# Feed-forward products of a spectral-mixing and SwiGLU kernel: float32 products with block sums and Strassen, against three float32r products of 12-bit parts in stripes of 512 tokens

## Chip, core and metric

The kernel runs on one core of one Trainium2 chip. The metric is the device time of one execution in microseconds (us). Three runs of the kernel before gave 2791.26, 2792.60 and 2793.78 us, so its median is 2792.6 us.

Engine names are those of the profile: PE is TensorE (matrix products), PEld its weight loads, DVE is VectorE, ACT is ScalarE, POOL is GpSimd, SP is SyncE, which only issues DMAs here.

## What is computed

```python
batch, seq, dim = 8, 3008, 256
d_ff = 1536
X = np.fft.rfft(x, axis=1)                       # x: (8, 3008, 256) float32
y = np.fft.irfft(X * (filt_r + 1j * filt_i)[None], n=seq, axis=1)
x2 = y.astype(np.float32).reshape(8 * 3008, 256)  # 24064 tokens
g = x2 @ w_gate                                   # 256 x 1536
h = g * (1.0 / (1.0 + np.exp(-g))) * (x2 @ w_val)
out = (h @ w_out).astype(np.float32)              # 1536 x 256
```

The three weight matrices arrive as 64-bit floats and are turned into 32-bit ones on the chip.

## The kernel before

**Spectral part.** For each of the 8 batches the transforms are short products with tables of sines and cosines, with twiddle and filter factors between them. Batch 0 runs first, alone, in stages written out by hand: `stage1_first`, `turn`, `stage2a`, `stage2b`, `stage3` (L896 to L1026). Its result is needed in four chunks (`NCHUNK`), and the feed-forward part starts when chunk 0 is there. Each later batch is transformed while the feed-forward part of the batch before it runs; its products are bursts of small matmuls: `quads` (tile wqa, L727), `fours` (wqb L819 there, wqc L807 home) and `back` (wpd, L1043). Batch 1 still uses an older path (`stage1`, `stage2a`, `stage2b`).

**Feed-forward part.** `Group` (L1091) is one chunk of a batch with a third of the hidden units: 96 groups. The tokens of a chunk stand in four classes, and the weights in four blocks. The hidden products are taken of sums of token classes and of weight blocks (`P`, `Q`, `A`, `B`, `E` in `product`, L1118, matmuls at L1125): 26 products for the gate half and 26 for the value half, each a matmul of 128x128 weights with 188 columns of float32. DVE, ACT and POOL form the sums before and after (`f`, `c`, `D`, `x`, `y`, `m`, `l`, `s`, `e`). The output product is a Strassen scheme: seven products of 128x128 with 376 columns, each over two blocks (`project`, L1223, 14 matmuls a group), with sums of hidden tiles (`S`, on POOL, L312 and L315) before and additions into the output (`o`, DVE L312) behind.

**Weights.** `round_half` (L386) turns one half of a weight block from 64-bit to 32-bit floats with DVE, ACT and POOL operations of 128x256 elements (DVE: L395, L398, L418, L422). `Preparation` spreads these operations over the first groups. The finished sums of weights are kept in DRAM and a third of them is loaded again for every group (`reload_weights`, tile wt_t from w_all).

**Order.** All engines run their instructions in program order; `pin` keeps that order. The order inside a group is the hand-written list `SCHEDULE`: each token is one operation of this group, of the one before it, or one step of a spectral piece. DMAs are nearly all issued by SP, in program order.

Two helpers hide what an operation is for: `add` (L312) and `sub` (L315) issue sums on the engine that they are given, `negated_sum` (L319) one DVE operation. A matmul of float32 shows as two MATMUL records in the trace.

Of the kernel before, what the change touches and what calls it, by code (L numbers as in the profile page):

```python
# [12 lines left out]
FP32 = mybir.dt.float32  # L42
U32 = mybir.dt.uint32
# [7 lines left out]
NM = DFF // 128  # L51
NJ = NM // 2
# [6 lines left out]
NH = 4  # L59
NW = 2 * NH  # L60
NCHUNK = 32 // NW
TH = NH * NR
RP = 96
NT = 3
NG = 3
JB = NJ // NG
TQ = TH // 2
NB = 8
# [9 lines left out]
WO = {1: 0, 7: 1, 2: 2, 3: 3, 5: 4, 6: 5, 4: 6}  # L78
HID = {1: 0, 6: 6, 4: 2, 2: 3, 5: 4, 7: 1, 3: 5}

SCHEDULE = """
Q0 o3' z1.o' t4.2' W2 b0 f0 S00' S01' i0 b1 b2 x0.o' t0.0 x1.o' i1 Q1 P0 t0.1 x2.o' P3 x3.o' f1 t4.3'
W1 x4.o' S10' x03 S11' D01 i2 i3 i4 s13 b3 x5.o' P1 o1 b4 t0.2 o2 z0.o c1 i5 A13 g1 c0 S20' Q2  # L90
S21' g0 y01 m13 t1.0 h0 f2 s01 W6 t1.1 h1 x23 D02 P2 o6 D12 A01 t0.3 i6 c2 i7 B13 i8 g2 i9 n3' m01
i10 S30' t1.2 i11 x02 W7 S31' g13 y12 y02 B01 h13 o7 t1.3 t2.0 s02 s12 g01 h2 b5 Q3 t2.1 h01 e12
A02 y23 W4 e02 b6 y03 m02 g3 A12 o4 z2.o t2.2 E12 m12 B02 t2.3 l12 e13 b7 E02 u12 g02 t3.0 h3 s23
l02 B12 v12 E13 t3.1 h02 u02 A23 n2 l13 g12 v02 W5 s03 e23 h12 e01 m23 A03 o5 z3.o u13 E23 t3.2 m03
v13 E01 l23 e03 t3.3 t4.0 l01 u23 B23 v23 u01 E03 n1 t4.1 v01 g23 B03 l03 W3 h23 g03 u03 h03 v03
""".split()
KS = (-1, 0, 1, 2)

LAST = """
S00 S01 W1 S20 S21 S10 S11 W2 o1 W5 o2 S30 S31 W6 o5 o6 W4 W7 q4 o4 z2.o x0.o x1.o x2.o x3.o x4.o x5.o  # L100
o7 W3 o3 z1.o X0.o X1.o X2.o X3.o X4.o X5.o
""".split()
FILTER_AT = ("f1", "P0", "Q2", "h0")
BLOCKS = (0, 1, 3, 2)
PAIRS = ((0, 1), (1, 2), (2, 3), (0, 2), (1, 3), (0, 3))
PAIRS_USED = ((1, 3), (0, 1), (0, 2), (1, 2), (2, 3), (0, 3))
ORDER = [t for t in SCHEDULE if t[0] in "PQABE"]
VIA_SBUF = {t[1:] for t in SCHEDULE if t[0] == "x" and t[1:].isdigit()}, \
    {t[1:] for t in SCHEDULE if t[0] == "y"}
SLOT = {p: i for i, p in enumerate(ORDER)}  # L110
SUM = {f"{z}{i}{j}": 6 * e + n for e, z in enumerate("ABE") for n, (i, j) in enumerate(PAIRS)}
NPR = len(ORDER)

LATER = N1 - 32

PIECES = ((0, 7), (7, 14), (14, 20), (20, 26))

def dft_tables():
# [45 lines left out]
    for t in range(NS):  # L168
        u, at = divmod(t, 4)
        for e in range(2):  # L170
# [11 lines left out]
    thc = th - np.where(n2 < 32, 0.0, 1.0)[:, None, None] * 2 * np.pi * s / (2 * N1)  # L182
    c, sn = np.cos(thc), np.sin(thc)
    turned = np.zeros((2, N2, NS, 2, NQ))
    turned[0, :, :, 0] = c.transpose(0, 2, 1)
    turned[1, :, :, 0] = sn.transpose(0, 2, 1)
    turned[0, :, :, 1] = (-sn * sg).transpose(0, 2, 1)
    turned[1, :, :, 1] = (c * sg).transpose(0, 2, 1)
    turned = turned.reshape(128, NS, 128).transpose(2, 1, 0)

    pairs = np.arange(128).reshape(2, N2).T.ravel()
    later = np.stack([de[:, :, 0], turned[:, :, pairs]], 2)
    f32 = np.float32
    wf = np.pad(wf.reshape(NR, NK), ((0, 0), (0, 128 - NK)))
    return (wf.astype(f32), wi.reshape(NK, NR).astype(f32),
            back.astype(f32), quad.astype(f32), four.astype(f32), np.ascontiguousarray(de).astype(f32),
            np.ascontiguousarray(later).astype(f32))
# [3 lines left out]
def kernel(  # L201
# [11 lines left out]
    wf_host, wi_host, back_host, quad_host, four_host, de_host, later_host = dft_tables()  # L213
# [6 lines left out]
    later_dram = nc.inline_tensor(later_host, name="later_tbl").ap()  # L220
    unit_dram = nc.inline_tensor(np.eye(128, dtype=np.float32), name="unit_tbl")

    def pool(name, bufs, space=None):
# [4 lines left out]
    xpool = pool("xp", 2)  # L228
    t1pool = pool("t1", 2)
    t4pool = pool("t4", 2)  # L230
    ypool = pool("yp", 2)
    wdpool = pool("wdram", 1, DRAM)
    wps = pool("wps", NB, PSUM)

    wf_t = cpool.tile([NR, 128], FP32)
    wi_t = cpool.tile([NK, NR], FP32)

    wt_t = cpool.tile([128, NPR, 2, 128], FP32)
    y_t = cpool.tile([128, 3 * len(PAIRS), TQ], FP32)

    lent = cpool.tile([128, 14 * NV * C], FP32)
    wt_1 = lent[:, 0:NPR * 256].rearrange("p (s z f) -> p s z f", z=2, f=128)
    places = {"t2": (0, 2, 1), "f": (2, 2, 2), "tb": (6, 3, 1), "p": (9, 2, 1), "q": (11, 1, 1),
              "g": (12, 2, 1)}

    def lend(tag, u):

        first, count, units = places[tag]
        a = (first + u % count * units) * NV * C
        return lent[:, a:a + units * NV * C].rearrange("p (i c) -> p i c", c=C)  # L250

    fours = {"x": (0, 2, 2), "f": (0, 4, 1), "y": (4, 2, 1), "g": (6, 2, 1), "e": (8, 2, 1),
             "t": (10, 2, 1), "tb": (12, 1, 1)}
# [7 lines left out]
    def weights_of(b, k, g):  # L261
        return wt_1 if b == 0 and k < NT and g == 1 else wt_t

    dram_tiles = [wdpool.tile([2 * NS, N2, C], FP32, name=f"d{1 + i % 2}_{i // 2}")
                  for i in range(4)]
    quads_dram = [wdpool.tile([64, N2, C], FP32, name=f"quads_{i}") for i in range(2)]
    turned_dram = [wdpool.tile([16, 128, C], FP32, name=f"turned_{i}") for i in range(2)]
    yt_dram = [wdpool.tile([128, 3 * len(PAIRS), TQ], FP32, name=f"yt_{k}") for k in range(NT)]
# [55 lines left out]
    def weight_halves():  # L324
# [8 lines left out]
        def hid(g, i):  # L333
            for z in range(2):
                yield cols[z][JB * g + i // 2][:, i % 2], ("hid", g, i, z)
# [1254 lines left out]
```

## Time and profile before

| what | value |
|---|---|
| median of 3 runs | 2792.6 us |
| profiled execution, span from first to last instruction | 2788.6 us (4.0 us under the median) |
| granted TensorE clock, mean | 0.997 of full speed |
| busy: PE, DVE, POOL, ACT | 99%, 75%, 59%, 54% |
| first feed-forward product starts | 76.1 us |
| PE matmuls of line L1125 (hidden products), records | 9984 in the six largest groups |
| DMA | 608.47 MB, mean 218 GB/s |
| weights loaded again (wt_t from w_all) | 174 loads of 896 KB, 174 of 768 KB |

The span is the time of one profiled execution, and the sums of the prediction are made against it. A group of instructions in the page is given as line, engine, operation, output and input tiles, shape and count, then busy time (overlaps counted once) and mean duration of one in ns. In the timeline the first column is the start in us, the second the length of a merged run of equal instructions. Instructions of one engine overlap a little, so that what one costs in a dense stream is the distance of starts, not its duration.

### The profile page before, as it was taken

The numbers are of one execution on the slowest core, as the hardware profiler recorded it, in microseconds if no ns is written. First come the engines' busy times: TensorE is split into PE (matmuls) and PEld (weight loads), VectorE is DVE, ScalarE is ACT, GpSimd is POOL, SyncE is SP. The second block draws the span as 40 slices with busy tenths as digits, with TensorE's granted clock in tenths as the row PEclk, the third lists the DMA queues.
The fourth block names the chain that finished last, engine by engine and source line by source line (L and its number), as shares of the span: only waits on it lengthen the run. The fifth ranks groups of instructions, "written<-read, shape, count | busy, mean of one in ns | idle before, by whom it ended". The sixth has DMA issues, their size and how long they took to land.

```text
span 2788.6 us, 51410 instructions
## 1 busy us (share of the span) xinstructions
PE 2748.3 (99%) x16952; PEld 2249.3 (81%) x16952; DVE 2081.7 (75%) x4703; ACT 1514.6 (54%) x4086; POOL 1647.4 (59%) x1801
## 2 busy tenths in 40 slices
PE   8999999999999999999999999999999999999998
PEld 6777887888878888788878888878887888888886
DVE  7888777777687777777778777777777777676666
ACT  5776454555555555555555555555554555555553
POOL 4786576566545665556654566555655566555554
PEclk9999999999999999999999999999999999999999
DMA  8688877878676776777767777668767677655543
GB/s 216 218 273 267 282 240 243 265 243 263 205 211 208 253 244 190 212 238 229 247 184 233 220 249 223 207 194 264 243 213 201 215 239 237 183 156 147 156 137 83
DMA packets 383488, 608.47 MB, mean 218 GB/s; under 512 B 197118, under 2 KB 266652, under 8 KB 383048
## 3 DMA queue, kind: packets, MB, share of 16 engines
q1 hardware_dynamic: 364410, 574.18, 65.9%
q10 hardware_dynamic: 16174, 25.50, 3.6%
q0 software_dynamic: 2640, 5.51, 0.7%
q8 instruction: 137, 2.24, 0.3%
q14 instruction: 127, 1.04, 0.1%
HBM read 484.45 MB, written 118.12 MB: 216 GB/s over the span
## 4 chain that ended last, share of the span: by engine, by line
PE 89%; DVE 3%; POOL 2%; ACT 1%; DMA 1%; issue 1%; SPq 0%; POOLq 0%; DVEq 0%; ACTq 0%
PE wa L1125 25%; PE wk L1125 17%; PE wA L1223 16%; PE we L1125 12%; PE wG L1223 8%; PE wF L1223 4%; PE wpd L1043 2%; PE wqc L807 1%; PE wqb L819 1%; PE wqa L727 1%; POOL h L315 0%; POOL out_dram L1208 0%; PE wpa L889 0%; DVE we L315 0%; DVE y L319 0%
## 5 line engine op out<-in xcount | busy, mean ns | idle before, releaser
L1125 PE MATMUL wa<-y_t,wt_t 128*128 128x188 f32 x4464 | 883.5, 324 | 10.5 <-DVE wa L1147 5.5
L1125 PEld LDWEIGHTS wa<-y_t,wt_t 128*128 128x128 f32 x4464 | 746.0, 190 | 102.9 <-issue 14.7
L1125 PEld LDWEIGHTS wk<-y,wt_t 128*128 128x128 f32 x2976 | 494.4, 190 | 125.2 <-issue 36.7
L1125 PE MATMUL wk<-y,wt_t 128*128 128x188 f32 x2976 | 575.6, 326 | 1.4 <-ACT f L1140 1.4
L315 POOL TENSOR_TENSOR h<-h 128x376 f32<-128x376 f32 x572 | 560.1, 1000 | 15.1 <-DVE h L312 14.9
L1223 PE MATMUL wA<-h,wo_t 128*128 128x376 f32 x1532 | 549.0, 481 | 3.4 <-POOL h L315 1.8
L1125 PE MATMUL we<-y_t,wt_t 128*128 128x188 f32 x2232 | 432.4, 323 | 2.4 <-DVE we L319 1.6
L315 POOL TENSOR_TENSOR D<-f,f 128x376 f32<-128x376 f32 x288 | 280.5, 985 | 252.0 <-ACT f L1140 245.4
L312 POOL TENSOR_TENSOR h<-h 128x376 f32<-128x376 f32 x190 | 183.2, 984 | 408.0 <-DVE h L1172 402.2
L315 DVE TENSOR_TENSOR we<-we,m 128x376 f32<-128x376 f32 x576 | 317.3, 552 | 91.6 <-PE we L1125 51.4
L1125 PEld LDWEIGHTS we<-y_t,wt_t 128*128 128x128 f32 x2232 | 369.1, 190 | 4.9 <-DVE we L319 2.8
L1223 PEld LDWEIGHTS wA<-h,wo_t 128*128 128x128 f32 x1532 | 278.0, 190 | 106.6 <-POOL h L315 5.4
L1160 ACT COPY m<-wa 128x376 f32<-128x376 f32 x576 | 275.4, 478 | 110.8 <-PE wa L1125 105.0
L1167 ACT ACTIVATE u<-we 128x188 f32<-128x188 f32 x576 | 188.9, 328 | 188.5 <-DVE we L315 179.1
L1223 PE MATMUL wG<-h,wo_t 128*128 128x376 f32 x768 | 273.9, 479 | 0.0
L319 DVE SCALAR_TENSOR_TENSOR y<-wk,c 128x376 f32<-128x376 f32 x480 | 246.7, 540 | 33.7 <-ACT c L1144 29.5
L1167 ACT ACTIVATE g<-wa 128x188 f32<-128x188 f32 x576 | 187.4, 326 | 143.8 <-PE wa L1125 141.6
L1144 ACT COPY c<-wk 128x376 f32<-128x376 f32 x288 | 136.9, 475 | 234.5 <-PE wk L1125 228.1
L1156 ACT COPY we<-y 128x376 f32<-128x376 f32 x480 | 218.9, 480 | 42.9 <-DVE y L1049 24.7
L1140 ACT ACTIVATE f<-wk 128x376 f32<-128x376 f32 x288 | 145.1, 504 | 168.6 <-PE wk L1125 108.3
L1172 DVE TENSOR_TENSOR h<-we,u 128x188 f32<-128x188 f32 x576 | 198.7, 345 | 35.1 <-ACT u L1167 21.9
L1172 DVE TENSOR_TENSOR h<-wa,g 128x188 f32<-128x188 f32 x576 | 196.1, 344 | 26.2 <-ACT g L1167 26.1
(194 smaller groups left out, 3532.0 us busy)
## 6 DMA issues: line engine op xcount, KB each, us to landing
wt_t<-w_all SPq DMA_DIRECT2D x174, 896.0 KB
wt_t<-w_all SPq DMA_DIRECT2D x174, 768.0 KB
lent<-filter SPq DMA_DIRECT2D x36, 1024.0 KB
quads<-lent SPq DMA_DIRECT2D x96, 256.0 KB
d<-lent ACTq DMA_DIRECT2D x84, 256.0 KB
t<-d SPq DMA_DIRECT2D x112, 192.0 KB
lent<-quads SPq DMA_DIRECT2D x144, 128.0 KB
lent<-raw SPq DMA_DIRECT2D x144, 128.0 KB
```

The source lines that it names most:

```text
L312: return eng.tensor_tensor(out=dst, in0=a, in1=b, op=ALU.add)
L315: return eng.tensor_tensor(out=dst, in0=a, in1=b, op=ALU.subtract)
L319: return nc.vector.scalar_tensor_tensor(out=dst, in0=a, scalar=-1.0, in1=b, op0=ALU.mult, op1=ALU.subtract)
L1043: pin(nc.tensor.matmul(out=outs_[h][32 * j:32 * j + 32, i], lhsT=back_t[0][r, ts(m, 32)], rhs=t[r, j], start=i == 0, stop=True, skip_group ...
L1125: pin(nc.tensor.matmul(out=ps[:, z], lhsT=self.wt[:, SLOT[p], z], rhs=rhs, start=start and z == 0, stop=True, skip_group_check=True))
L1140: pin(act.mul(self.small(f"f{i}", f"f{i}", 1), t[f"k{i}"], -1.0))
L1144: pin(act.copy(out=self.small(f"c{i}", f"c{i}", 1), in_=t[f"k{i}"]))
L1156: pin(act.copy(out=self.bank(f"e{at}"), in_=t[f"y{at}"]))
L1160: pin(act.copy(out=self.small(f"m{at}", "m", 4), in_=t[f"a{at}"]))
L1167: pin(act.activation(out=self.small(op, "g", 3, 1)[:, 0], in_=ps[:, 1], func=AF.Silu))
L1172: pin(v.tensor_tensor(out=dst, in0=ps[:, 0], in1=g, op=ALU.mult))
L1223: pin(nc.tensor.matmul(out=self.tiles[at], lhsT=wo_t[:, JB * q + i, WO[p], :], rhs=self.hs[i][:, HID[p]], start=start and i == 0, stop=Tru ...
```

## The change

The spectral part keeps its arithmetic, and every batch from 1 on uses `quads`, `there`, `home` and `back` (the path of the later batches before). The feed-forward part is written anew:

- The tokens are cut into 47 stripes of 512 (`T`), without regard to batches; the result of the spectral part stands in one tile `y_t` of a whole batch.
- Each value that enters a product is cut into an upper part of 12 bits (`hi`), the rest (`lo`), and a third number `both` that is the upper part minus 4096 times the rest; for weights `both` is `hi - lo` with `lo` already scaled. With p = `hi·hi` + `lo·lo` and s = `both·both` the whole product is p (1 + 1/4096) - s / 4096. They are matmuls of float32r tiles with 512 columns: 6 for the gate, 6 for the value and 6 for the output in each unit. A `Unit` is one stripe with 128 hidden units: 47 x 12 = 564 units, 10152 matmuls.
- Per unit DVE has four operations of 128x512 (gate combined, value combined, product of both, `both` of the hidden tile), ACT four (two scaled copies from PSUM, Silu, `hi`), POOL one subtraction (`lo`).
- The first five stripes are passed three times with a third of the hidden units each (60 units, `EARLY_UNITS`), while the weights are prepared at three ticks a unit (`preparation.tick`). Partial outputs go through DRAM and are joined on POOL.
- From unit 60 on half of the weight tiles stay in SBUF; the other six (`STREAM`) are loaded again for each stripe: 250 loads of 768 KB (gate and value) and 250 of 384 KB (output).
- All four chunks of batch 0 are finished (`stage3`, 16 steps) ahead of the first unit.
- The order is a loop over units; spectral pieces, splits of the next stripe and stores hang at places a, b, c, p of given units (`hooks`).

The core of the diff; the new line numbers are those of the changed kernel.

```diff
-SCHEDULE = """
-Q0 o3' z1.o' t4.2' W2 b0 f0 S00' S01' i0 b1 b2 x0.o' t0.0 x1.o' i1 Q1 P0 t0.1 x2.o' P3 x3.o' f1 t4.3'
...
-    class Group:
...
+        pin(nc.gpsimd.tensor_tensor(out=w, in0=w, in1=pf, op=ALU.mult))
+        yield
+        t = gv_t[slot_of(d)][:, z] if z < 2 else wo_t[slot_of(d)]
+        hi, lo, both = [t[:, :, n] for n in range(3)]
+        pin(scaled(hi, w, DOWN / LAM))
+        yield
+        pin(axpy(lo, hi.bitcast(FP32), -LAM, w))
+        yield
+        pin(sub(nc.gpsimd, both, hi.bitcast(FP32), lo.bitcast(FP32)))
...
+        TIMES = (0, 1, 2, 3, 4, 5, 6, 7, 8, 10, 11)
...
+            for i, (_, d, z) in enumerate(weights):
+                b = 4 * i
...
+    def split_y(key, a, src, first, last, fast=False):
...
+        pin(scaled(hi, src, DOWN))
+        pin(sub(nc.vector if fast else nc.gpsimd, lo, src, hi.bitcast(FP32)))
+        return lambda: pin(axpy(both, lo.bitcast(FP32), -LAM, hi.bitcast(FP32)))
...
+        def hidden(self, z):
+            w, (yh, yl, yb) = gv_t[self.slot][:, z], ys[self.key]
+            s, p = bank(f"s{z}_{self.n}"), bank(f"x{z}_{self.n}")
+            for a in range(2):
+                pin(nc.tensor.matmul(out=s, lhsT=w[:, a, 2], rhs=yb[:, a], start=a == 0,
+                                     stop=a == 1, skip_group_check=True))
+            for a in range(2):
+                for n, t in enumerate((yh, yl)):
+                    pin(nc.tensor.matmul(out=p, lhsT=w[:, a, n], rhs=t[:, a], start=a + n == 0,
+                                         stop=a + n == 2, skip_group_check=True))
+            return s, p
+        def gate(self):
+            s, p = self.hidden(0)
+            pin(scaled(self.g, s, 1.0 / LAM))
+            pin(axpy(self.g, p, BOTH, self.g, ALU.subtract))
+        def value(self):
+            s, p = self.hidden(1)
+            pin(scaled(v, s, 1.0 / LAM))
+            pin(nc.scalar.activation(out=self.g, in_=self.g, func=AF.Silu))
+            pin(axpy(p, p, BOTH, v, ALU.subtract))
+            pin(nc.vector.tensor_tensor(out=self.h, in0=p, in1=self.g, op=ALU.mult))
+        def split(self):
+            pin(scaled(self.hs[0], self.h, DOWN))
+            pin(sub(nc.gpsimd, self.hs[1], self.h, self.hs[0].bitcast(FP32)))
+        def split_rest(self):
+            pin(axpy(self.hs[2], self.hs[1].bitcast(FP32), -LAM, self.hs[0].bitcast(FP32)))
+        def project(self, c):
+            w, (hi, lo, both) = wo_t[self.slot], self.hs
...
+            p, s = outs[2 * c], outs[2 * c + 1]
+            pin(nc.tensor.matmul(out=s, lhsT=w[:, c, 2], rhs=both, start=self.first,
+                                 stop=self.last, skip_group_check=True))
+            pin(nc.tensor.matmul(out=p, lhsT=w[:, c, 0], rhs=hi, start=self.first,
+                                 stop=False, skip_group_check=True))
+            pin(nc.tensor.matmul(out=p, lhsT=w[:, c, 1], rhs=lo, start=False,
+                                 stop=self.last, skip_group_check=True))
...
+    def evacuate(u, c):
+        pin(scaled(o, s, 1.0 / LAM))
+        pin(axpy(o, p, BOTH, o, ALU.subtract))
...
+    for u, v in zip(items, items[2:]):
+        at(u.n + 1, "a", lambda v=v: pin(nc.sync.dma_start(out=gv_t[v.slot].bitcast(FP32), in_=gv_dram[v.d].bitcast(FP32))))
+        at(u.n + 3, "a", lambda v=v: pin(nc.sync.dma_start(out=wo_t[v.slot].bitcast(FP32), in_=wo_dram[v.d].bitcast(FP32))))
...
+    for n in range(NU + 2):
+        u, one_back, two_back = unit_at(n), unit_at(n - 1), unit_at(n - 2)
...
+        run_hooks(n, "a")
+        preparation.tick(n)
+        if one_back:
+            one_back.split()
+        if two_back:
+            two_back.split_rest()
+        run_hooks(n, "b")
+        preparation.tick(n)
+        if u:
+            u.gate()
+            u.value()
+        run_hooks(n, "c")
+        preparation.tick(n)
+        if two_back:
+            two_back.project(0)
...
+        run_hooks(n, "p")
+        if two_back:
+            two_back.project(1)
```

`axpy` is one DVE scalar_tensor_tensor, `scaled` one ACT copy with a factor, and `bank` gives one of four PSUM banks in turn to the units' products and to the spectral bursts; the outputs of a stripe hold the other four (`ops`). The gate, the value and the product read PSUM; `split_rest` and the `both` of `split_y` read two SBUF tiles.

## The prediction

> **What bounds the kernel now.** I read the busy shares first, then the chain that ended last, then the timeline of PE in the middle of the run. The first two are:
>
> ```profile
> PE 2748.3 (99%) x16952; PEld 2249.3 (81%) x16952; DVE 2081.7 (75%) x4703; ACT 1514.6 (54%) x4086; POOL 1647.4 (59%) x1801
> ...
> PE 89%; DVE 3%; POOL 2%; ACT 1%; DMA 1%; issue 1%; SPq 0%; POOLq 0%; DVEq 0%; ACTq 0%
> ```
>
> PE is never idle and carries 89% of the chain, so the time is the sum of PE's work, if matmuls stream without holes. The timeline of PE tells whether they do (start, length, engine, line):
>
> ```profile
> 1506.49 0.80 PE L1125 MATMUL wa<-y_t,wt_t 128*128 128x188 f32 x4
> 1507.13 0.80 PE L1125 MATMUL we<-y_t,wt_t 128*128 128x188 f32 x4
> 1507.77 0.80 PE L1125 MATMUL wa<-y_t,wt_t 128*128 128x188 f32 x4
> 1508.40 1.43 PE L1223 MATMUL wG<-h,wo_t 128*128 128x376 f32 x4
> 1509.66 0.80 PE L1125 MATMUL wk<-y,wt_t 128*128 128x188 f32 x4
> 1510.30 1.43 PE L1223 MATMUL wF<-h,wo_t 128*128 128x376 f32 x4
> 1511.66 1.14 PE L727 MATMUL wqa<-lent,quad 24*32 24x512 f32 x32
> 1512.73 0.59 PE L1125 MATMUL wk<-y,wt_t 128*128 128x188 f32 x2
> ```
>
> The distance of starts is the price: four records of 188 columns in 0.64 us, four of 376 in 1.26, that is 0.159 and 0.316 a record: 0.0024 fixed and 0.835 ns a column. Weight loads (PEld) hide under that. A float32 product is two records: 0.318 us at 188, 0.632 at 376. A group costs 52 x 0.318 + 14 x 0.632 = 25.4 us, and the 96 groups 2437 of the 2788.6 us.
>
> **What the change does to PE.** It issues 10152 products of 512 columns. No row shows a float32r matmul. [...] Ends of the range: 0.216 and 0.430. [...]
>
> A unit is then 18 x 0.216 = 3.89 us of PE. Spectral bursts stay as they are: wqa 1.07 us (row above), wpd 1.03, wqb 0.97, wqc 0.92 by distances of starts, for a batch 4 x 1.07 + 8 x 1.03 + 6 x (0.97 + 0.92) = 23.9 us.
>
> **What the others must do in 3.89 us.** Nearest rows for 128x512, in the groups by form (line, engine, operation, tiles, shapes, count, busy, mean ns, idle before):
>
> ```profile
> L837 DVE TENSOR_TENSOR lent<-wqb,lent 128x512 f32<-128x512 f32 x72 | 49.2, 683 | 12.2 <-ACT raw L833 12.2
> ...
> L842 ACT COPY lent<-wqc 128x512 f32<-128x512 f32 x36 | 21.1, 586 | 63.3 <-PE wqc L807 63.3
> ...
> L877 POOL TENSOR_TENSOR lent<-lent 128x512 f32<-128x512 f32 x48 | 60.4, 1278 | 1.3 <-DMA lent<-raw 1.3
> ```
>
> DVE has four operations a unit, ACT four, POOL one: 4 x 0.683 = 2.73, 4 x 0.586 = 2.34, 1.28 us. Back to back a DVE operation costs 0.61 (two L837 rows and their successors start 0.60 and 0.61 apart), so 2.44. Per stripe DVE adds about six (two each for evacuation, transposition, `both` of y), per batch some 52 spectral ones. For 72 units: 288 x 0.683 + 36 x 0.7 + 52 x 0.69 = 258 us with durations, 231 back to back; PE has 280 + 24 = 304. So PE stays the bound, with DVE at 76 to 85%.
>
> The longest loop over engines is also shorter than a unit: h ready, ACT `hi` 0.59, ACT gate copy 0.52, DVE gate 0.69, ACT Silu 0.59, DVE product 0.69, and four hand-overs of 0.1 (ACT u ends 2769.07, DVE h starts 2769.16): 3.5 us. Behind the gate's DVE operation, which now waits for ACT, stand value, product and the next unit's `split_rest`; the outputs are multiplied two units late, so PE waits only if all this slips by more than the 1.3 us until a PSUM bank is needed again.
>
> **What speaks against it** is `split_rest`, a DVE operation with both inputs in SBUF while POOL works. The end of the timeline shows the pair:
>
> ```profile
> 2770.25 1.00 DVE L312 TENSOR_TENSOR h<-h 128x376 f32<-128x376 f32 x2
> 2770.94 2.40 POOL L315 TENSOR_TENSOR h<-h 128x376 f32<-128x376 f32 x2 [14.87 <-DVE h L312]
> 2771.17 2.57 DVE L315 TENSOR_TENSOR h<-h 128x376 f32<-128x376 f32 x2
> ...
> 2774.77 1.00 DVE L315 TENSOR_TENSOR h<-h 128x376 f32<-128x376 f32 x2
> ```
>
> Alone two of them take 1.00 us, beside POOL 2.57, and POOL's own go from 1.00 to 1.20 each. Operations that read PSUM do not feel it: L837 keeps 0.68 beside POOL. At 512 columns the loss is 0 to 1.0 us for each of 86 such operations in 72 units. In a plain unit `split_rest` runs while ACT still makes `hi`, ahead of POOL's subtraction, and escapes; with spectral work on POOL (20 of 72 units have two to four more operations) it does not. I take 0.3 on average, 26 us a batch, still under PE's 304. [...]
>
> **The first 60 units** are where DVE, not PE, is the bound. The weights' preparation runs beside them: 36 half blocks, about nine done by the first unit, the other 27 over 37 units (three ticks a unit, four a half block). DVE has five operations for each; the fourth of them, L422, shows both prices (min/median/max ns):
>
> ```profile
> L422 DVE SCALAR_TENSOR_TENSOR w<-raw,w x8: 420/1066/1218, 130.0 to 273.6; 128x256 f32<-128x256 uint32 x8
> ...
> L422 DVE SCALAR_TENSOR_TENSOR lent<-raw,lent x2: 418/418/418, 123.9 to 221.1; 128x256 f32<-128x256 uint32 x2
> ```
>
> By mean rows (0.60, 0.61, 0.62, 0.94, 0.64, less 0.08 of overlap each) a half block is 3.0 us, 1.5 without POOL beside it. A unit of this phase needs on DVE 3 x 0.61 + 1.25 (`split_rest`, between 0.61 and 1.66, as POOL is some 80% busy here) + 0.5 (y) + 0.3 (evacuation) + 0.47 (spectral) + 0.75 x 3.0 (weights) = 6.6 us, against 3.89 on PE. So 37 x 6.6 = 244, and the other 23 units 89 + 12 of bursts: 345 us. If nothing contends it is 274, if all does 380.
>
> **Start and end.** The first product came at 76.1 us. Now 12 more steps of `stage3` lie ahead of it, 0.87 us apart on PE, and the split of the first stripe (ACT 0.59, DVE 0.69 and 0.61, hand-overs), 2.5: 89, rounded to 90. Chunks 1 to 3 must also come back from DRAM, 2.4 MB, so up to 100. After the last matmul (2779.6 us in the timeline) the before needs 9 us; I keep 9.
>
> **DMA** costs nothing here: 250 x 1152 KB replace 174 x 1664 KB, 295 against 296 MB. The page's slices reach 282 GB/s, the mean of the new kernel would be 235. A weight load waits on SP until PE has read the slot, with the spectral loads queued behind it, and is due three units (11.7 us) later. Without that cover each stripe would lose a few us.
>
> **The sum:** 90 + 345 + 504 x 3.89 (1960) + 6 x 23.9 (143) + 9 = 2547, and 2% of the 1823 us with spectral work (36) for units that slip further than the PSUM banks allow, between 0 and 235 (the second rival): 2583. The profiled execution lies 4 us under the median: **2587 us**, 7.4% less than 2792.6.
>
> **Rivals.**
> - PE is the bound from the first unit on: preparation and `split_rest` fit into gaps. 90 + 60 x 3.89 + 24 + 1960 + 143 + 9 + 4 = 2463. For it: PE is 29 to 30 of 30 us busy from 120 us on in the before, preparation included. Against: the sum of 6.6 us above.
> - VectorE becomes the bound everywhere, through POOL: all `split_rest` and y operations pay 0.97, and nothing overlaps. A batch is 258 + 86 x 0.97 = 341, the start phase 380: 90 + 380 + 6 x 341 + 280 + 9 + 4 = 2809, slower than before. It is slower from 0.9 us of loss per operation on. For it: 2.57 against 1.00. Against: the plain units, where POOL is idle when it runs.
> - float32r is no single pass (the change does not do what it says): at one record's 0.430 us the units alone are 564 x 7.74 = 4365, the total about 4630.
>
> **How the numbers follow.** Forecast 0.65 (2500 to 2700), first rival 0.16, second 0.13 (of which 0.03 ends between 2700 and 2787 and 0.01 within the limit), third 0.06. Faster by more than 0.2%, about what a measurement of this kernel tells from no change: 0.65 + 0.16 + 0.03 = 0.84; within 0.01; slower 0.09 + 0.06 = 0.15. The range holds forecast and first rival, 0.81: 2455 to 2730.
>
> **What would show it.** Right: MATMUL rows of 512 columns 0.216 us apart; PE above 95% busy from some 440 us on and near 60% between 90 and 330; DVE near 100% there; `split_rest` (one line with all `axpy`, tile hs) around 0.7 to 1.0 us mean, the PSUM readers at 0.68. Wrong: distances near 0.43; DVE on the chain after 440 us; PE waiting for weight loads (DMA gv); a first product later than 105 us.

## The result, and the profile after

The changed kernel takes 3017.4 us (median of four runs, 3014.99 to 3020.4), the kernel before 2791.9 beside it: 1.0815 times as long (95% interval 1.080 to 1.083). The forecast was 2587, with a range of 2455 to 2730. The profiled execution has a span of 3014.4 us, 431 more than the 2583 of the sum.

Busy shares, the granted clock by slices, and the chain that ended last, from the page after:

```profile
PE 2828.9 (94%) x14620; PEld 2062.6 (68%) x14620; DVE 2380.7 (79%) x3210; ACT 1614.8 (54%) x2907; POOL 1526.0 (51%) x1153
...
PEclk8688899999999999999999999999999999999999
...
PE 53%; DVE 9%; DMA 8%; issue 7%; POOL 6%; SPq 2%; ACT 2%; DVEq 0%; POOLq 0%; ACTq 0%
```

PE is still the busiest engine, but it now has holes: 53% of the chain where it had 89%; the rest of the chain runs over DVE, POOL, ACT and transfers, for which PE waits. The granted clock is below 0.9 in the first five of the forty slices (377 us). "Busy" is no measure of PE's work here: neighbouring records overlap (0.39 us long and 0.23 apart in the rows below), so the distance of starts has to be read. PE's timeline late in the run, where no transform is left:

```profile
2800.13 0.39 PE L928 MATMUL o_s<-hs,wo 128*128 128x512 f32 x1
2800.36 0.40 PE L930 MATMUL o_s<-hh,wo 128*128 128x512 f32 x1
2800.60 0.39 PE L932 MATMUL o_s<-hl,wo 128*128 128x512 f32 x1
2800.83 0.39 PE L928 MATMUL o_s<-hs,wo 128*128 128x512 f32 x1
2801.07 0.40 PE L930 MATMUL o_s<-hh,wo 128*128 128x512 f32 x1
2801.30 0.39 PE L932 MATMUL o_s<-hl,wo 128*128 128x512 f32 x1
```

One record a product, 0.23 us apart (median of the dense ones 0.232, most single distances 0.226 to 0.238). So float32r takes one record where float32 takes two, but not at 0.216.

The operations that the prediction priced, from the groups of the page:

```profile
L229 POOL TENSOR_TENSOR hl<-h,hh 128x512 fp32r<-128x512 f32 x564 | 765.6, 1357 | 1302.0 <-ACT hh L232 1240.6
...
L235 DVE SCALAR_TENSOR_TENSOR hs<-hl,hh 128x512 fp32r<-128x512 f32 x564 | 601.2, 1066 | 15.0 <-POOL hl L229 14.1
L235 DVE SCALAR_TENSOR_TENSOR wx<-wx,v 128x512 f32<-128x512 f32 x564 | 391.2, 694 | 191.4 <-PE wx L892 169.2
```

DVE's readers of PSUM (wx) cost 0.69 us as forecast; `split_rest` (hs) 1.07, that is 0.38 lost on average where 0.3 was taken. DVE at 79% is not the bound of the whole run; in the first 60 units, though, it is busy for 368 of 408 us.

Time by stage is read from the starts of Silu (L906), one for each unit. Forecast and measured terms, in us:

| term | forecast | measured | difference |
|---|---|---|---|
| first feed-forward product | 90 | 132.5 | +42 |
| first 60 units | 345 | 408 | +63 |
| 504 units without transforms, each | 3.89 | 4.256 | 504 x 0.366 = +185 |
| what the transforms add in six batches (bursts 143, slips 36) | 179 | 6 x (358.9 - 72 x 4.256) = 315 | +136 |
| from first product to first Silu, and the end | 9 | 14 | +5 |
| sum | 2583 | 3014 | +431 |

The 4.256 is the mean of the last 72 units, beside which no transform runs; 358.9 is the mean of the six batches of 72 units before.

### The profile page after: what moved, and what is told of

Its sections match the earlier page's. It is cut to its first block, busy times and chain, and to the rows that moved or that the text cites. A ratio compares the mean times of both kernels' runs of the same rounds, so it can differ in the third digit from the quotient of the medians.

```text
span 3014.4 us, 44431 instructions
## 1 busy us (share of the span) xinstructions
PE 2828.9 (94%) x14620; PEld 2062.6 (68%) x14620; DVE 2380.7 (79%) x3210; ACT 1614.8 (54%) x2907; POOL 1526.0 (51%) x1153
## 4 chain that ended last, share of the span: by engine, by line
PE 53%; DVE 9%; DMA 8%; issue 7%; POOL 6%; SPq 2%; ACT 2%; DVEq 0%; POOLq 0%; ACTq 0%
PE wx L892 20%; PE ws L888 11%; PE o_s L928 6%; PE o_s L930 5%; PE o_s L932 5%; DVE hs L235 3%; DMA gv<-gv_all 2%; PE wqa L586 2%; POOL hl L229 2%; DMA lent<-d 2%; POOL yl_s L229 1%; DVE lent L693 1%; POOL lent L226 1%; SPq L404 1%; PE wpd L740 1%
## 5 line engine op out<-in xcount | busy, mean ns | idle before, releaser
L229 POOL TENSOR_TENSOR hl<-h,hh 128x512 fp32r<-128x512 f32 x564 | 765.6, 1357 | 1302.0 <-ACT hh L232 1240.6
L892 PE MATMUL wx<-yh_s,gv 128*128 128x512 f32 x2016 | 801.9, 398 | 2.9
L892 PE MATMUL wx<-yl_s,gv 128*128 128x512 f32 x2016 | 797.2, 395 | 0.0
L888 PE MATMUL ws<-ys_s,gv 128*128 128x512 f32 x2016 | 640.4, 398 | 21.1 <-DMA gv<-gv_all 8.7
L235 DVE SCALAR_TENSOR_TENSOR hs<-hl,hh 128x512 fp32r<-128x512 f32 x564 | 601.2, 1066 | 15.0 <-POOL hl L229 14.1
L235 DVE SCALAR_TENSOR_TENSOR wx<-wx,v 128x512 f32<-128x512 f32 x564 | 391.2, 694 | 191.4 <-PE wx L892 169.2
L906 ACT ACTIVATE g<-g 128x512 f32<-128x512 f32 x564 | 354.4, 628 | 326.0 <-DVE g L235 323.0
L888 PEld LDWEIGHTS ws<-ys_s,gv 128*128 128x128 f32 x2016 | 379.4, 189 | 121.0 <-issue 14.9
L892 PEld LDWEIGHTS wx<-yh_s,gv 128*128 128x128 f32 x2016 | 381.0, 189 | 107.9 <-DVE h L909 14.9
L928 PE MATMUL o_s<-hs,wo 128*128 128x512 f32 x1008 | 427.1, 424 | 18.3 <-DVE hs L235 9.3
L909 DVE TENSOR_TENSOR h<-wx,g 128x512 f32<-128x512 f32 x564 | 390.3, 692 | 60.2 <-DVE wx L235 1.4
L930 PE MATMUL o_s<-hh,wo 128*128 128x512 f32 x1008 | 399.1, 396 | 0.0
L932 PE MATMUL o_s<-hl,wo 128*128 128x512 f32 x1008 | 396.8, 394 | 0.0
```

Of the source, the lines that this page charges most:

```text
L229: return eng.tensor_tensor(out=dst, in0=a, in1=b, op=ALU.subtract)
L235: return nc.vector.scalar_tensor_tensor(out=dst, in0=a, scalar=scale, in1=b, op0=ALU.mult, op1=op)
L888: pin(nc.tensor.matmul(out=s, lhsT=w[:, a, 2], rhs=yb[:, a], start=a == 0, stop=a == 1, skip_group_check=True))
L892: pin(nc.tensor.matmul(out=p, lhsT=w[:, a, n], rhs=t[:, a], start=a + n == 0, stop=a + n == 2, skip_group_check=True))
L906: pin(nc.scalar.activation(out=self.g, in_=self.g, func=AF.Silu))
L909: pin(nc.vector.tensor_tensor(out=self.h, in0=p, in1=self.g, op=ALU.mult))
```

## The experiments

The total is the time of one execution of each (for the changed kernel the median); the kernel before took 2787 to 2797 us beside them. The stages of each, in us, by the starts of Silu:

| run | total | first Silu | first 60 units | batch of 72 | last units, each |
|---|---|---|---|---|---|
| the changed kernel | 3017.4 | 136.7 | 408 | 358.9 | 4.256 |
| no_spectral | 2634.4 | 136.2 | 337 | 307.2 | 4.25 |
| no_preparation | 2972.4 | 122.4 | 377 | 359.2 | 4.25 |
| no_preparation_no_loads | 2926.9 | 112.1 | 349 | 358.0 | 4.25 |
| bare_units | 2540.2 | 111.6 | 267 | 307.3 | 4.25 |
| loads_ahead | 3006.6 | 123.8 | 407 | 359.6 | 4.25 |
| start_warm | 2992.1 | 111.4 | 409 | 359.0 | 4.25 |
| one_burst | 3078.8 | 136.4 | 415 | 368.1 | 4.26 |
| subtraction_on_dve | 2976.3 | 135.0 | 406 | 353.8 | 4.19 |
| rest_on_act | 2933.0 | 135.6 | 372 | 352.1 | 4.18 |
| split_shifted | 2973.9 | 135.0 | 410 | 351.8 | 4.26 |
| all_three | 2944.9 | 113.1 | 401 | 353.1 | 4.18 |
| act_shift_start | 2876.2 | 118.1 | 372 | 345.5 | 4.18 |

### The distance of the products: three measurements

> Leaves the whole computation out; it only issues dense rows of matmuls, each kind into its own PSUM bank, with weights that change at every matmul as in the changed kernel: float32 of 512 columns (two records each), float32r of 512 accumulating, float32r of 512 each on its own, float32r of 256 and of 384 columns, float32r with 64 weight columns, float32r with a moving operand of zeros, bf16 of 512, and at the end float32r of 512 again beside copies of ACT and sums of DVE from PSUM. In the changed kernel two float32r products of 512 columns start 0.232 us apart where 0.216 was predicted. (a) If the 0.016 us is a fixed cost of a matmul: 0.232 at 512, 0.179 at 384, 0.125 at 256 columns, alone as well as beside other engines. (b) If it is a rate of 0.453 ns a column: 0.174 at 384, 0.116 at 256. (c) If the change of weights costs it: 64 weight columns give 0.216, and bf16 weights too. (d) If the engines beside PE cost it: 0.216 alone, 0.232 only in the last row. (e) If the numbers themselves cost it (clock granted by switching): zeros give 0.216 and the other rows 0.232. float32 is expected at 0.430 a record.

```diff
+    run(24, banks[0], w_f, m_f)
+    run(48, banks[1], w_r, m_r)
+    run(48, banks[3], w_r, m_r, cols=256)
+    run(48, banks[4], w_r, m_r, cols=384)
+    run(48, banks[6], w_r, z_r)
+    run(48, banks[7], w_b, m_b)
...
```

Groups of the measurement by form (count, busy time, mean ns of one):

```profile
L107 PE MATMUL b<-z_r,w_r 128*128 128x512 f32 x48 | 11.1, 389 | 0.0
L107 PE MATMUL b<-m_b,w_b 128*128 128x512 bf16 x47 | 10.3, 379 | 0.1
L107 PE MATMUL b<-m_r,w_r 128*128 128x384 f32 x48 | 8.5, 334 | 0.0
L107 PE MATMUL b<-m_r,w_r 128*128 128x256 f32 x48 | 5.9, 283 | 0.0
```

In a dense row the distance is (busy - one duration) / (count - 1): for bf16 (10.3 - 0.379) / 46 = 0.216, for float32r of 256 columns (5.9 - 0.283) / 47 = 0.120. By the single starts float32r has 0.227 at 512 columns, 0.1734 at 384, 0.120 at 256: 0.418 ns a column and 0.013 us fixed. So (a), the fixed cost, holds against (b); half as many weight columns gave 0.230, so not (c), although bf16 weights go with 0.216 as (c) also said; PSUM copies beside it left 0.227 by the single starts (and m3_waits, below, has 72 products in 16.5 us beside ACT's copies, 0.227 each), so not (d); zeros gave 0.227, so not (e). But the expected 0.232 did not come: alone it is 0.227. float32 came at 0.429 a record as expected, 0.858 a product, about four times the bf16 row.

> Leaves the whole computation out; dense rows of float32r matmuls again. The first measurement gave 0.227 us at 512 columns, 0.1734 at 384 and 0.120 at 256, that is 0.418 ns a column and 0.013 us fixed (bf16: 0.216), while the changed kernel has 0.232. Rows here: one weight tile and one moving tile throughout; moving tile changing over four; both changing; 128 and 320 columns with one tile each; the order of the changed kernel (two products into one bank, four into another, tiles changing); and at the end both changing again with loads from DRAM into other tiles beside it. Theory (fixed cost): 0.066 at 128 columns (0.0535 + 0.013) unless the load of weights, 0.188 us a record, sets a floor near 0.09; 0.147 at 320. For the missing 0.005 us: if the change of the moving tile costs it, 0.232 in the rows where it changes and 0.227 where it does not; if the change of the bank costs it, 0.232 only in the kernel's order; if transfers cost it, only in the last row.

```diff
+    row(48, banks[0], same_w, same_m)
+    row(48, banks[1], same_w, some_m)
+    row(48, banks[2], some_w, some_m)
+    row(48, banks[3], same_w, same_m, 128)
+    row(48, banks[4], same_w, same_m, 320)
+    kernel_order(8, banks[5], banks[6])
...
```

0.147 at 320 columns, as the fixed cost says; 0.111 at 128, above the expected 0.066 and above the 0.09 at which the weight loads (0.188 us a record) were expected to set a floor; what sets it was not tried. At 512 columns every row had 0.227: neither the tiles, nor the kernel's order, nor transfers beside it bring 0.232. The first products had 0.427 (the granted clock is 0.962 on average over the run), the distance of the changed kernel's products at a granted clock of 0.50 (median of 179). That is twice 0.2135, and 512 x 0.418 ns is 0.214: no fixed cost shows in these.

> Leaves the whole computation out; dense float32r products of 512 columns, with a PSUM bank that changes every 24, 4 and 2 products and is waited for and copied out (a quarter of its columns) by ACT, and again every 4 with sums of POOL, and of DVE, on tiles in SBUF beside it. Undisturbed rows had 0.227 us between starts, whatever tiles they used; the changed kernel has 0.232, with single distances of 0.226 to 0.238. Theory (each change of bank with its wait for a semaphore brings matmul and weight load out of step, and some products take 0.231 to 0.238 until they are in step again): 0.227 in the row of 24, 0.230 to 0.233 with 4 and with 2. Rivals: POOL's or DVE's traffic in SBUF costs it, then only those two rows stand above 0.229; or neither, then all rows are at 0.227.

```diff
+    row("long", 3, 24)
+    row("four", 18, 4)
+    row("two", 36, 2)
+    row("pool", 18, 4, nc.gpsimd)
+    row("dve", 18, 4, nc.vector)
```

All rows 0.227, those with waits at every second product and those with POOL or DVE beside them too. This theory fell, and so did the first of its rivals, traffic of POOL or DVE; the row of values that came is that of the last one, under which neither costs it. What brings the kernel from 0.227 to 0.232 stays open; it is worth 0.005 x 10152 = some 50 us.

### Without the transforms of batches 1 to 7

> Leaves out the transforms of batches 1 to 7: the feed-forward part multiplies batch 0's result eight times over. All 564 units, the preparation of the weights and the start stay. Theory (spacing 0.232 and bursts with waits around them): a unit from 60 on takes 4.20 to 4.28 us everywhere, as the last 72 of the changed kernel, so 504 units take 2117 to 2157 us; the first 60 units lose their bursts and part of POOL's work and take 340 to 390; with the first unit still near 136 the total is 2600 to 2700 us. Rival (the units themselves are bound by DVE's two-SBUF operations beside POOL): the batches of units stay above 4.6 us a unit, and the total above 2850.

```diff
-    for b in range(1, B):
+    for b in range(1, 1):
```

307.2 us for 72 units, 4.27 each, total 2634: theory right. So the units themselves stream with PE as the bound, at 18 x 0.232 = 4.18 and 0.09 of waits, and the transforms cost 358.9 - 307.2 = 51.7 us a batch, where 23.9 + 6 of slips were forecast. The first 60 units fell to 337, just under the 340 to 390 expected. The edit also takes the transforms' work off DVE, ACT, POOL and SP, so that the 51.7 us are bursts and waits together.

### One burst in place of two

> Same computation; the two bursts of 8 small products of quads are issued as one burst of 16, as in the kernel before, into all four PSUM banks of the pool at once. In the kernel before 16 of them took 1.07 us, in the changed one 8 take 1.02 undisturbed and 1.42 on average. Theory (products on different quarters of the array run side by side, so a burst costs the same with 8 as with 16): one burst of about 1.1 us in place of two, 4 x 1.0 to 4 x 1.8 us less a batch, total 20 to 50 us less than 3016. Rival (four banks at once leave the units without banks, and PE waits for the copies out of them): PE waits 1 to 2 us more behind each burst, and the total is the same or up to 30 us more.

```diff
-            burst(0)
+            burst()
...
-            burst(1)
-            yield
+            yield
```

61 us slower, worse than the rival's 30. PE's timeline of the changed kernel, a half burst and the product behind it:

```profile
1275.09 1.09 PE L586 MATMUL wqa<-lent,quad_t 24*32 24x512 f32 x16
1276.11 0.50 PE L928 MATMUL o_s<-hs,wo 128*128 128x512 f32 x1
```

The same view of this run, the whole burst:

```profile
1297.22 2.22 PE L587 MATMUL wqa<-lent,quad_t 24*32 24x512 f32 x32
1299.37 0.50 PE L928 MATMUL o_s<-hs,wo 128*128 128x512 f32 x1
```

16 records (8 products) take 1.02 us to the next start; the kernel before had 32 records in 1.07 (the prediction's row at 1511.66): there 16 records of 0.61 us each start 7 ns apart, so that small products which the kernel places on different parts of the array run side by side. Cutting the burst in two therefore about doubles its price here, 2 x 1.02 us for 1.07. Here 32 records take 2.15: only the first three products start at 1297.22, all others at 1298.31 and behind, because the fourth bank is not free: DVE reads it for the product of both until 1298.26. The pool has no four free banks, and afterwards the units wait as well (PE waits 13.8 us for ACT's g copies and 9.2 for its v copies between 545 and 2760 us, neither among the nine largest waits of the changed kernel from 545 us on). The two halves are what four banks allow.

### The start

> Same computation; the loads of half blocks 9 and 10 of the weights are issued ahead of the six table loads, into room that is free, so that DVE does not wait 16 us (to 57.07) for half block 9 with the spectral steps of batch 0 behind it. Theory (this wait sets the start): the first unit starts 8 to 18 us earlier than 136, PE's hole between 38 and 58 us closes, total 2996 to 3008. Rival (the start hangs on the table loads and on the way of chunks 1 to 3 through DRAM): first unit within 4 us of before, total within 5 us of 3016.

```diff
-                ("x", 3), ("w", 5), ("w", 6), ("w", 7), ("w", 8)] + [("t", n) for n in range(6)]
+                ("x", 3), ("w", 5), ("w", 6), ("w", 7), ("w", 8), ("w", 9), ("w", 10)] + [("t", n) for n in range(6)]
```

DVE's waits between 20 and 70 us in the changed kernel (who for whom, us in total, times, longest):

```profile
DVE rt L275 <- DMA rt<-in_moe_w_gate_dram: 16.0, 1, 16.0
```

With the loads ahead this wait is gone, and the first unit comes 12.9 us earlier, the total 10.8: theory right.

> Same computation; the loads of half blocks 9 and 10 ahead of the tables, as before (that brought the first unit from 136.7 to 123.8 us), and more idle matmuls of zeros, 14 in place of 6 ahead of stage3 and 9 between its first and its second chunk, where PE waits for chunks from DRAM. There stage3 ran at 0.22 us a record, 128 records in 28 us, against 0.11 in the kernel before. Theory (the granted clock falls while PE waits, and stage3 pays it): stage3's records are 0.11 to 0.13 us apart, the first unit comes 6 to 12 us earlier than 123.8. Rival (the chunks' way through DRAM sets it): the waits between chunks grow by what the records lose, and the first unit comes within 3 us of 123.8.

```diff
-        idle(zero, 6)
+        idle(zero, 14)
         preparation.finish(0)
         for k in range(NCHUNK):
+            idle(zero, 9 * (k == 1))
```

PE's timeline of the changed kernel in `stage3`:

```profile
96.10 7.11 PE L525 MATMUL wpd<-wi_t,f 96*128 96x94 f32 x32 [7.82 <-DMA f<-room]
108.58 13.94 PE L525 MATMUL wpd<-wi_t,x 96*128 96x94 f32 x64 [5.36 <-DMA x<-d]
122.31 7.03 PE L525 MATMUL wpd<-wi_t,lent 96*128 96x94 f32 x32
```

The same view of this run:

```profile
81.50 3.78 PE L525 MATMUL wpd<-wi_t,f 96*128 96x94 f32 x32 [0.33 <-DMA f<-room]
85.12 7.92 PE L384 MATMUL widle<-room 128*128 128x512 f32 x18
93.36 7.35 PE L525 MATMUL wpd<-wi_t,x 96*128 96x94 f32 x64 [0.33 <-DMA x<-d]
100.55 3.74 PE L525 MATMUL wpd<-wi_t,lent 96*128 96x94 f32 x32
```

The same 64 records take 13.94 and 7.35 us. While PE waits for chunks from DRAM the granted clock falls to one half (0.50 between 92 and 130 us in the changed kernel), and idle matmuls keep it up (1.00 between 76 and 107 us in this run). First unit at 111.4, 12.4 us earlier again, slightly more than forecast. Between 111 and the forecast's 90 + 4 lies mostly the chunks' way through DRAM: the first chunk's product started at 81.5 (72.5 in the kernel before), the second's at 93.4, each right behind its load.

### The first 60 units

> Leaves out the conversion of the weights from 64-bit to 32-bit numbers: upper part and rest are two scaled copies on ACT of the high words, and POOL's subtraction stays, so that DVE has nothing to do for the weights and POOL one operation less. Theory (DVE's preparation is what the first 60 units wait for): they take 280 to 310 us where the changed kernel takes 410, and the total falls to 2880 to 2915 us. Rival (the spectral steps of batch 1 and the loop over hi, lo and both are what they wait for): still 350 us or more, total above 2955.

```diff
-        pin(v.tensor_scalar(out=man, in0=high, scalar1=0xFFFFF, scalar2=None,
...
-        pin(nc.gpsimd.tensor_tensor(out=w, in0=w, in1=pf, op=ALU.mult))
...
+        pin(scaled(hi, high, DOWN))
+        pin(scaled(lo, high, 2.0 ** -6))
```

377 us and a total of 2972, where the theory asked for 280 to 310: it fell, and the rival's numbers came. DVE is busy for 282 us of this phase where the changed kernel has 368, and 86 us less of its work bring only 31. The edit changes the work of ACT and POOL too, so the 31 are what the whole conversion is worth, not DVE's part alone. ACT's waits here between 125 and 545 us show one thing that took its place:

```profile
ACT wo L232 <- DMA rt<-in_moe_w_out_dram: 26.4, 8, 8.8
...
ACT gv L232 <- DMA rt<-in_moe_w_val_dram: 23.4, 5, 9.7
```

The loads stand in SP's queue among the transforms' loads and stores, each of which waits for an engine; and behind ACT's wait stand its copies out of PSUM.

> As the run without preparation, and without the loads of the weights too: upper part and rest are ACT copies of a constant tile, so that nothing in the preparation waits for a transfer. In the run without preparation ACT waited 50 us for half blocks of weights between 125 and 545 us, with the copies out of PSUM queued behind. Theory (those waits, caused by weight loads standing behind spectral transfers in SP's queue, are what replaced DVE's load there): the first 60 units fall from 377 to 300 to 335 us. Rival (spectral bursts and the order of the spectral steps bound them): 355 us or more.

```diff
         if i in raws or i >= len(weights):
-            return
+        return
...
-        high = raw[:, :, :, 1].bitcast(FP32)
+        high = some[:, 0:256].rearrange("p (b f) -> p b f", b=2)
```

349: between the two expectations. The loads are worth 28 us, and most of what is left is elsewhere.

> Leaves out the transforms of batches 1 to 7 and the conversion and loads of the weights (ACT copies of a constant tile and POOL's subtraction in their place). The first 60 units took 408 us in the changed kernel, 337 without transforms, 377 without DVE's preparation, 349 without preparation and loads. Theory (transforms and preparation together make the loss, by sharing the queues of DVE, ACT, POOL and SP): 255 to 285 us here, near 60 x 4.26. Rival (the three passes themselves, with a split of y and an evacuation every four units in place of every twelve, cost units): 295 us or more. A unit from 60 on stays at 4.26; total 2510 to 2580.

The edit is this one and that of no_spectral together. 267 us, as the theory said; the three passes with their splits and evacuations cost next to nothing (60 x 4.26 = 256). The windows show it (from and to, length, busy us and instructions of PE, PEld, DVE, ACT and POOL, granted clock, DMA share, GB/s). The changed kernel:

```profile
200.00:250.00 50.00, 36.00 (x142) 22.59 (x143) 44.84 (x58) 24.92 (x54) 34.99 (x29) 0.78 0.65 220
```

This run, the same stretch:

```profile
200.00:250.00 50.00, 49.59 (x213) 39.05 (x212) 41.45 (x59) 37.07 (x76) 37.49 (x30) 1.00 0.17 54
```

PE goes from 142 to 213 records in 50 us while DVE is nearly as busy as before. Added up: 267, + 82 for the transforms alone (349), + 70 for the weights alone (337), makes 419 for both, and 408 were measured. Each alone costs more than the 63 us by which the forecast missed this phase. PE's own waits between 136 and 545 us in the changed kernel name the place where both meet:

```profile
PE o_v L928 <- DVE hs L235: 50.7, 29, 4.9
```

It is not hl that hs waits for. In 35 of the 60 units PE takes hs within 0.2 us of its end; in all of them hl had been there for 2.0 to 8.7 us (median 5.7), and DVE worked right up to the start of hs. So hs stands in DVE's queue, behind work for the weights, the transforms and the units themselves. That transforms and weights add up because both fill this queue is read from these times, not tried by itself.

Part of it is again the clock: 136 of the feed-forward product records up to 545 us last over 0.55 us, at half clock. At 0.427 instead of 0.232 for each that is an estimate of at most 27 us.

### The way from h to hs

> Same computation; the subtraction that makes lo of the hidden tile goes from POOL to DVE, behind split_rest, so that in units without spectral work POOL stands still and DVE's operations with both inputs in SBUF are not slowed by it; DVE gets one operation more for each unit. Theory (DVE beside POOL is what makes the units slip): split_rest falls from 1.07 to 0.70 us mean, the early units from 408 to below 380 us, a batch from 359 to below 350, total below 2940. Rival (PE's own work and the order of the steps bound the batches; DVE's load is no matter or gets worse): batches 355 to 365 us, early units 400 or more, total 2990 or more.

```diff
-            pin(sub(nc.gpsimd, self.hs[1], self.h, self.hs[0].bitcast(FP32)))
+            pin(sub(nc.vector, self.hs[1], self.h, self.hs[0].bitcast(FP32)))
...
-        if one_back:
-            one_back.split()
         if two_back:
             two_back.split_rest()
+        if one_back:
+            one_back.split()
```

The two operations in this run's page:

```profile
L229 DVE TENSOR_TENSOR hl<-h,hh 128x512 fp32r<-128x512 f32 x564 | 539.6, 957 | 22.0
L235 DVE SCALAR_TENSOR_TENSOR hs<-hl,hh 128x512 fp32r<-128x512 f32 x564 | 454.4, 806 | 0.0
```

Engine and order change together here. hs falls from 1.07 to 0.81 us, yet the batch only to 353.8 and the early units to 406: total 2976, between the two expectations, nearer to the rival. The last units fall to 4.19, so most of the 0.08 above 18 x 0.232 were waits for hs: in the changed kernel's last units PE waits in the first two of each stripe, where DVE has the outputs of the stripe before in its queue ahead of hs and hs itself runs beside POOL (1.55 us on average), with hl there 3.2 us earlier or more. The next run leaves hl on POOL and comes to 4.18 as well.

> Leaves out a part: split_rest becomes a scaled copy on ACT, -4096 times lo without adding hi, so that DVE's only operation of a unit with both inputs in SBUF is gone (601 us of DVE's 2381) and ACT has one copy more. With the subtraction on DVE in place of POOL, split_rest had fallen from 1.07 to 0.81 us mean, a plain unit from 4.256 to 4.194, a batch from 359 to 354, but the first 60 units only from 408 to 405, DVE having got one operation more. Theory (DVE's queue, filled by work slowed beside POOL, sets the first 60 units and part of the waits around the bursts): the first 60 units take 340 to 375 us, a batch 343 to 352, total 2880 to 2940. Rival (PE's order, its bursts and the transfers): first 60 units 395 or more, batches 355 or more, total above 2980.

```diff
-            pin(axpy(self.hs[2], self.hs[1].bitcast(FP32), -LAM, self.hs[0].bitcast(FP32)))
+            pin(scaled(self.hs[2], self.hs[1].bitcast(FP32), -LAM))
```

Total 2933, first 60 units 372, batch 352.1: within the theory's numbers but for the batch, at their edge. DVE falls to 63%, and the total by 84 us. The edit brings hs earlier and takes 538 us of work off DVE; which of the two counts it does not tell. By distances of starts the six batches gain nearly all of their 41 us where PE takes hs.

> Same computation; the split of the next stripe's inputs is moved from the units 9 to 6 ahead of the stripe to the units 6 to 4 ahead, where POOL has no product and sum of the transform's filter step to make. In the changed kernel the halves of a stripe with these splits take 5.2 to 5.4 us a unit and the others 4.43. Theory (POOL's subtractions for y and for the filter step stand ahead of hl in one queue, and PE waits for what depends on hl): a batch falls from 359 to 345 to 353 us, total 2960 to 2990. Rival (the waits come with the bursts themselves, wherever the splits are): batches 357 to 362, total within 8 us of 3016.

```diff
-                split_at_unit(n - 9 + 2 * a, "b", key, a, y_t[:, a, s0:s0 + T])
+                split_at_unit(n - 6 + a, "b", key, a, y_t[:, a, s0:s0 + T])
```

Batch 351.8, total 2973.9: the theory's numbers came, and the rival falls. Moving nothing but the splits gives 43 us. The traces show another mechanism than the theory's, though. By distances of starts the six batches get 42.6 us shorter: 21.2 between the small products of wqc, 15.3 between those of wqa, and only 4.1 in front of the product that needs hs. PE's longest waits between 545 and 2700 us in the changed kernel are

```profile
PE wqc L653 <- POOL lent L226: 11.6, 18, 0.8
PE wqa L586 <- DVE g L235: 9.5, 6, 1.6
```

and neither appears in this run, while DVE waits for hl as much as before (12.6 and 13.7 us in the batches). So POOL's queue is the place, but what came late in it was not hl: in all 18 late bursts of wqc the split of y (1.74 us) ran on POOL just ahead of the filter step's sum, and the burst went on 0.05 us behind that sum. The waits of wqa end with DVE's reading of the gate, which frees a bank. A burst of wqc took 1.67 us on average and takes 1.08 here, one of wqa 1.43 and 1.10.

> Same computation; the loads ahead and idle matmuls of the start, the subtraction on DVE with split_rest ahead of it, and the shifted split, together. If the savings are independent they add: 13 and up to 10 us at the start, 41 from the subtraction on DVE, up to 50 from the shifted split, total 2900 to 2965. The floor of this form, 564 units of 4.18 us with bursts of 28 us a batch and the start, is 113 + 2358 + 196 + 9 = 2676; the kernel before stands at 2790, and I expect this one not to reach it.

The edits of start_warm, subtraction_on_dve and split_shifted together: 2944.9, within the expectation, but the savings do not add in the batches (353.1, above the 351.8 of the shift alone): with one operation more for each unit DVE is 89% busy.

> Leaves out a part: split_rest as a scaled copy on ACT, without adding hi, as in the run with the rest on ACT; with it the start (loads ahead, idle matmuls) and the shifted split. If the savings add, 2933 - 25 - 42 = 2866; since the shifted split and the lighter DVE both bring hl and hs earlier, I expect part of it twice: 2870 to 2910. It tells whether what the experiments found is enough to reach the kernel before at 2790; theory: it is not, as PE's own work with the products 0.232 us apart, the bursts and the start fill 2676.

The edits of start_warm, rest_on_act and split_shifted together: 2876.2 as expected, batch 345.5. It leaves out adding hi and still is 85 us above the kernel before.

## Why the prediction was wrong

- **A product at 0.216 us** is the step that cost most. No run shows this term, the author's estimate: undisturbed float32r rows showed 0.227, this kernel 0.232. One record a product came, at 0.232 and not at the third rival's 0.430. The 512 columns at the measured 0.418 ns are 0.214 us, so 0.216 leaves 0.002 for a fixed part, as float32's rows have it (0.0024); it is 0.013 us alone, with 0.005 more in this kernel. 18 x (0.232 - 0.216) x 564 = 162 us, of 206 that the forecast promised. What makes the 0.005 stays open. The prediction gave the distance a range up to 0.430, but its total took 0.216 as given.
- **"Spectral bursts stay as they are", 23.9 us a batch**: wrong twice. The change cuts the burst of quads in two, and by the rows the price is per burst (1.07 us with 16 products, 1.02 with 8), not per product: 4 x 1.0 us a batch, which the full diff showed. And the bursts bring waits: 51.7 us a batch in all, of which the 28 bursts themselves, undisturbed, are 28 x 1.02 = 28.6 (wqb and wqc are 1.02 as well, where 0.97 and 0.92 were taken). The other 23 were forecast at 6.
- **"Units that slip further than the PSUM banks allow", 2%**: the slips are there, 23 us a batch instead of 6, but only part of them come in the units. By distances of starts 8 lie inside bursts that wait for an operand or a bank (means of 1.43 for wqa, 1.20 for wqb, 1.67 for wqc), some 6 at the step into and out of each burst, about 0.10 us more each way, and the rest between the products of the units. Moving the splits saved 43 us, 37 of them inside the bursts; taking hs off DVE saved 84, 36 of them in the early units.
- **"The first 60 units", 345**: the term was 63 us too small, and its reason was half right. DVE is the busiest engine here, as forecast, and has somewhat more to do: 368 us, where the forecast's own prices (4.35 a unit without weights, 3.0 for each of 27 half blocks) make 342. The other 40 us are holes, which the sum put at nothing: it assumed that engines in order lose only what the busiest of them has to do. Leaving out the whole conversion brought 31 us with the loads left in and 59 without them, not the gain that a DVE bound would give; transforms (82) and weights (70) nearly add up.
- **"89, rounded to 90"**: 42 us late. Half block 9 of the weights on DVE, ahead of the spectral steps, 13; half clock in `stage3`, 12; the rest, some 17, is the chunks' way through DRAM, named as "up to 100" and dearer than that. That this last part is mostly theirs was read from the waits, not tried by an experiment. The 0.87 us for a step of `stage3` was a price at full clock (0.11 us a record in the kernel before), used where PE waits and the clock is 0.50 (0.213 a record).
- **split_rest at 0.3 us of loss**: right (0.38), as were the PSUM readers, and that DVE does not bound the steady state. The second rival, VectorE as the bound everywhere from 0.9 us of loss, is refuted, although its number, 2809, had the right sign: that is luck. For the first rival the prediction read PE as 29 to 30 of 30 us busy from 120 us on; the rows show 26.7 to 30.0.
- **DMA at nothing**: nearly right; loads of gv held PE for 8.7 us in six batches (16.0 in split_shifted).

Even with every other term as forecast, 4.256 a unit makes the sum 2583 + 185 = 2768, 0.7% below the kernel before: the distance took the gain, and the holes made the loss.

## What to carry to other kernels

When a change moves nearly all of an engine's work to a form that no row shows, every nanosecond of its price is multiplied by the count: put bounds on the fixed part as well, and let the range of the total follow from it. When a change brings PE's work per unit down to what the others need for it, a sum of each engine's work is no longer a forecast; follow the chain of each result through the queues (here h, hh, hl, hs, and the operands of the bursts), and ask what else stands ahead of it in each. Then check in the trace which link was late: here a forecast saving came in full through another link than the one named. Price a burst on part of the array by its own row before cutting it: here 8 small products took 1.02 us and 16 took 1.07, so two halves cost nearly twice the whole.

## What the runs showed of the hardware

- float32r of 512 columns: 0.227 us from start to start in undisturbed rows (0.013 us fixed, 0.418 ns a column), 0.111 at 128 columns; 0.427 at 512 columns where the granted clock was 0.50 (changed kernel, median of 179 distances); bf16 of 512 columns 0.216. In the kernel 0.232, cause open.
- A burst of 8 small products on 32-column strips takes 1.02 us to the next start, one of 16 took 1.07.
- DVE's operation hs, with both inputs in SBUF, takes 0.667 to 0.693 us in the 230 of 564 cases that no POOL operation overlaps, and 1.33 on average in the other 334, with a longest of 1.826. The mean of all is 1.07; in no_spectral, where POOL has less to do, it is 0.84, in subtraction_on_dve 0.81.
- The granted clock was 0.50 in `stage3` (92 to 130 us) and between 0.78 and 0.91 in the four stretches of 50 us from 150 to 350 us, where PE had holes of a few us. The 128 records of `stage3` took 28.1 us so, and 14.9 in start_warm, where idle matmuls keep the clock at 1.00: its first unit came 12.4 us earlier. For the first 60 units the loss is an estimate of at most 27 us (136 records, 0.427 in place of 0.232).
